# Later weight stores, a second PSUM bank for one transpose, and a moved ones product in an attention and feed-forward kernel

## The chip, the cores and the metric

The kernel runs on one core of a Trainium2 chip. The metric is device time in microseconds (us).

## The reference

Eight batches of attention with normalised queries and keys (12 heads, 448 positions, width 64), then a feed-forward block with squared ReLU, all in fp32 (the weights are handed in as doubles).

```python
def attention(q, k, v, g_q, g_k):            # (8, 12, 448, 64)
    rmsnorm = lambda x, g: x / np.sqrt(np.mean(x * x, axis=-1, keepdims=True) + 1e-06) * g
    scores = np.matmul(rmsnorm(q, g_q), rmsnorm(k, g_k).transpose(0, 1, 3, 2)) / np.sqrt(64)
    attn = np.exp(scores - np.max(scores, axis=-1, keepdims=True))
    return np.matmul(attn / (np.sum(attn, axis=-1, keepdims=True) + 1e-09), v)

x = attention(...).transpose(0, 2, 1, 3).reshape(3584, 768)
h = np.maximum(x @ w_in, 0.0)                # w_in (768, 2048)
return (h * h) @ w_out                       # w_out (2048, 768)
```

## The kernel before

The heads are worked through in pairs; a "pair" below is two heads of one batch, and pairs 0 to 11 are the first two batches. They run alone, by `attention_alone`. At the same time the weights are converted from doubles, block by block, in steps of a quarter tick ("prepare" has four parts, divided by `yield`), and each finished pair of blocks is stored to DRAM, seven sums and differences of it together (1344 KB). From then on the two matrix products of two batches at a time run on TensorE, with attention of the next two batches between the matmuls of the second product. The products fetch their weight blocks (192 KB) from DRAM into five buffers.

```python
def prepare(t):                                   # tick t
    if t == 0: unsigned(0)
    n = t - 3                                     # first quarter: the store of blocks n-1, n
    if there(n) and n % 2:
        c = n % NFC // 2
        dst = w1s[c] if n < NFC else w2s[:, c // 4, :, c % 4]
        nc.sync.dma_start(dst.rearrange("k p m -> p k m"), blocks_of(n)[:, 0:7])
        written[0] = n + 1
    # ... cut: clamp of the exponents of t on VectorE
    yield
    # ... cut: low words on ScalarE, shift on VectorE, first loads
    yield
    # ... cut: merge of bits on VectorE
    total(t - 2, S3, A11, A21, ALU.subtract)      # GpSimd; total() is for odd n only
    total(t - 2, S4, A12, S2, ALU.subtract)
    value(t - 1, 0)                               # GpSimd
    yield
    unsigned(t + 1)                               # ScalarE
    value(t - 1, 1)
    total(t - 1, S1, A21, A22, ALU.add)
    total(t - 1, S2, S1, A11, ALU.subtract)
    load_words(t, t - 1)                          # SP queue
    yield

def transpose(i, s, n):                           # n: which of two PSUM banks
    pt = bank("pt", n)
    for j in range(NJ):
        nc.tensor.transpose(pt[:, j * SP:(j + 1) * SP], normed[i][s][:, j * P:(j + 1) * P], ident[:SP, :SP])
    # ... cut: ScalarE copies pt to qkT

def values(i, chunks=range(NJ)):                  # pav of an odd pair lies in bank 1
    if 0 in chunks:
        pavs[i] = ps_o.tile([P, S], F32, tag="o", name="pav") if i >= NAT or i % 2 == 0 else bank("pav", 1)
    # ... cut: two matmuls for each chunk

def attention_alone():                            # NAT = 12 pairs
    for i in range(NAT):
        more = i + 1 < NAT
        if 0 < i < NAT - 3: load(i + 3)
        scores(i, 0)
        scores(i, 1)
        # ... cut: pair 0
        if more: transpose(i + 1, 1, 0)
        values(i - 1, (2, 3))
        add_up(i, 1)                              # VectorE
        if i + 2 < NAT: norm(i + 2)
        elif not more:
            norm(NAT)
            load(NAT + 2)                         # pair 14, waits until pair 12 is used
        yield                                     # after each yield: a step or two of prepare
        if more: transpose(i + 1, 0, 0)
        load_v(i + 1)
        yield
        scores(i, 2)
        scores(i, 3)
        total_of(i - 1)                           # the ones product: sums of the rows
        values(i, (0, 1))
        finish(i - 1)
        yield
        if added(i) == 3: add_up(i, 2)
        combine_x(i - 1)
        if NAT <= i + 3 < NAT + 2: load(i + 3)
        yield
    values(i, (2, 3))
    total_of(i)
    finish(i)
    combine_x(i)

for u, _ in enumerate(attention_alone()):         # EARLY = 52 steps, 13 ticks
    weights(min(EARLY, 4 + (EARLY - 4) * u // (4 * NAT - 7)))
    if u == 4 * NAT - 9:
        load_blocks(5)                            # the first five weight blocks of the product
```

## Time and profile before

| | before |
|---|---|
| time, median of the first 3 runs | 1401.57 us |
| span of the profiled run | 1399.7 us |
| TensorE busy | 1379.2 us (99%) |
| 75 to 115 us: GpSimd busy | over 19.5 of each 20 us |
| second weight block of the first product starts | 138.18 us |

A line of the timeline reads: start, duration, engine, source line, operation, output and input by name, shapes, count, and in brackets how long the engine was idle before it and what ended that. PE is TensorE, DVE VectorE, ACT ScalarE, POOL GpSimd, SPq the queue from which SP issues transfers. The trace counts each fp32 matmul twice: a weight block of three matmuls is x6.

In the names, pt is a transpose of queries or keys, sc the scores, tot the ones product, pav the values product, pa to pd the sums of the first product, sw a weight block, w1s and w2s the stored weights in DRAM; gT and gC hold probabilities, their sums and weights under conversion until the products need them.

### The profile page before, as it was taken

What the parts mean: (1) busy time and instruction counts of PE and PEld (TensorE: products, weight loads), DVE (VectorE), ACT (ScalarE), POOL (GpSimd) and SP (SyncE); (2) the same over time, 40 slices, a digit from 0 to 9 for tenths busy, and PEclk for the clock granted to TensorE, in tenths of its full rate; (3) what the DMA queues carried; (4) which work ended last, traced back from release to release, by engine and by line L of the source; (5) the groups of instructions that cost most, each with busy time, mean ns of one, the idle gap of its engine ahead of it and who ended that gap; (6) DMA issues with size and microseconds to landing.
All of it is one profiled execution on the core that took longest, in us unless ns stands there. A gap on an engine that the chain in (4) does not pass through costs nothing.

```text
span 1399.7 us, 14445 instructions
## 1 busy us (share of the span) xinstructions
PE 1379.2 (99%) x4450; PEld 638.5 (46%) x4450; DVE 802.2 (57%) x1398; ACT 419.6 (30%) x621; POOL 581.7 (42%) x400
## 2 busy tenths in 40 slices
PE   8989999999999999999999999999999999999997
PEld 3333455444444454544444455444444445554553
DVE  6889676589876234476777523457777633332111
ACT  7875556432322011233332011233333201110000
POOL 5998877444552123544453122544445302221000
PEclk9999999999999999999999999999999999999999
DMA  9687998545764332344665333344564332334443
GB/s 240 189 229 199 341 384 306 143 97 120 144 121 105 102 90 85 104 113 110 127 130 119 97 94 90 98 106 105 129 126 102 95 101 85 90 87 104 106 111 70
DMA packets 430915, 188.79 MB, mean 135 GB/s; under 512 B 277484, under 2 KB 428780, under 8 KB 430828
## 3 DMA queue, kind: packets, MB, share of 16 engines
q1 hardware_dynamic: 421228, 179.05, 49.8%
q10 hardware_dynamic: 9472, 8.72, 2.3%
q8 instruction: 38, 0.62, 0.2%
q14 instruction: 49, 0.40, 0.1%
q0 software_dynamic: 128, 0.00, 0.0%
HBM read 154.54 MB, written 33.16 MB: 134 GB/s over the span
## 4 chain that ended last, share of the span: by engine, by line
PE 93%; POOL 3%; DVE 1%; DMA 1%; ACT 1%; issue 1%; ACTq 0%; POOLq 0%
PE ps L1047 37%; PE sc L749 10%; PE pd L1000 10%; PE pa L1000 10%; PE pc L1000 10%; PE pav L805 9%; PE pb L1000 5%; PE tot L819 1%; POOL rstd L697 1%; POOL gC L563 1%; DMA sw<-w1s 1%; POOL gC L569 1%; PE pt L737 0%; ACT gT L754 0%; POOL qk L699 0%
## 5 line engine op out<-in xcount | busy, mean ns | idle before, releaser
L1047 PE MATMUL ps<-gT,sw 128*128 128x448 f32 x768 | 299.2, 543 | 0.8 <-POOL gT L977 0.8
L719 POOL TENSOR_TENSOR half<-half,mhalf 128x28 f32<-128x28 f32 x36 | 173.6, 4822 | 266.9 <-DVE half L718 226.8
L1047 PE MATMUL ps<-gC,sw 128*128 128x448 f32 x576 | 225.2, 543 | 0.0
L977 POOL TENSOR_TENSOR gT<-gT 128x448 f32<-128x448 f32 x96 | 94.9, 990 | 309.9 <-ACT gT L973 309.9
L1047 PEld LDWEIGHTS ps<-gT,sw 128*128 128x128 f32 x768 | 144.1, 190 | 150.7 <-issue 147.0
L756 ACT ACTIVATE pr<-sc 112x896 f32<-112x896 f32 x120 | 104.7, 914 | 293.4 <-PE sc L749 184.9
L749 PE MATMUL sc<-qkT 64*112 64x448 f32 x768 | 170.6, 563 | 0.9 <-ACT qkT L383 0.8
L1047 PEld LDWEIGHTS ps<-gC,sw 128*128 128x128 f32 x576 | 108.2, 190 | 112.1 <-issue 110.8
L1000 PE MATMUL pa<-xT,sw 128*128 128x448 f32 x384 | 154.9, 540 | 0.0
L973 ACT ACTIVATE gT<-gT 128x448 f32<-128x448 f32 x96 | 55.3, 577 | 310.1 <-DVE gT L1015 310.0
L749 PEld LDWEIGHTS sc<-qkT 64*112 64x112 f32 x768 | 61.2, 173 | 97.9 <-issue 81.3
L1000 PEld LDWEIGHTS pa<-xT,sw 128*128 128x128 f32 x384 | 73.0, 190 | 71.6 <-issue 70.3
L805 PE MATMUL pav<-pr,vt 112*64 112x448 f32 x480 | 100.2, 547 | 0.0
L721 POOL TENSOR_TENSOR qk<-qk,half 128x448 f32<-128x448 f32 x72 | 81.3, 1150 | 2.8
L764 DVE TENSOR_TENSOR acc<-acc,pr 112x896 f32<-112x896 f32 x60 | 68.2, 1136 | 21.0 <-ACT pr L756 18.5
L1000 PE MATMUL pb<-xC,sw 128*128 128x448 f32 x192 | 77.6, 540 | 1.5 <-issue 1.5
L1000 PE MATMUL pd<-xT,sw 128*128 128x448 f32 x192 | 77.9, 542 | 0.0
L1000 PE MATMUL pc<-xC,sw 128*128 128x448 f32 x192 | 77.5, 540 | 0.2 <-DMA sw<-w1s 0.2
L1000 PE MATMUL pd<-xC,sw 128*128 128x448 f32 x192 | 77.5, 540 | 0.0
L1000 PE MATMUL pc<-xT,sw 128*128 128x448 f32 x192 | 77.4, 539 | 0.0
L1015 DVE TENSOR_TENSOR gT<-z,pd 128x448 f32<-128x448 f32 x32 | 19.8, 620 | 99.7 <-PE pd L1000 99.7
L569 POOL TENSOR_TENSOR gC<-gC 128x384 f32<-128x384 f32 x64 | 72.8, 1157 | 2.5
(120 smaller groups left out, 1551.0 us busy)
## 6 DMA issues: line engine op xcount, KB each, us to landing
sw<-w1s SPq DMA_DIRECT2D x224, 192.0 KB, 2.3
sw<-w2s SPq DMA_DIRECT2D x168, 256.0 KB, 3.3
w1s<-gC SPq DMA_DIRECT2D x8, 1344.0 KB, 7.5
w2s<-gC SPq DMA_DIRECT2D x8, 1344.0 KB, 7.6
out_dram<-osb SPq DMA_DIRECT2D x184, 56.0 KB, 1.9
qk<-in_q_dram SPq DMA_DIRECT2D x144, 56.0 KB, 3.0
qk<-in_k_dram SPq DMA_DIRECT2D x144, 56.0 KB, 2.9
vt<-in_v_dram SPq DMA_DIRECT2D x72, 112.0 KB, 2.9
```

The source lines that it names most:

```text
L569: nc.gpsimd.tensor_tensor(*[blocks_of(n)[:, i] for i in (dst, x, y)], op)
L719: nc.gpsimd.tensor_tensor(half, half, mhalf, ALU.pow)
L721: nc.gpsimd.tensor_tensor(qkn[:, s], raw[:, s], half[:, s * NG:(s + 1) * NG].rearrange("p g -> p g ()").to_broadcast([P, NG, 32]), ALU.mult)
L749: nc.tensor.matmul(sc[:, h, 0:S], qkT[rows, at, 1, c * SP:(c + 1) * SP], qkT[rows, at, 0, :], start=True, stop=True)
L756: nc.scalar.activation(pr, sc[:, :, 0:S], AF.Exp)
L764: nc.vector.tensor_tensor(acc, probs[i, 0] if c == 1 else acc, probs[i, c], ALU.add)
L805: nc.tensor.matmul(pavs[i][h * D:(h + 1) * D, :], vs[i][:, h, c, :], probs[i, c][:, h, :], start=(c == 0), stop=(c == NJ - 1))
L973: nc.scalar.activation(g, src, AF.Relu)
L977: nc.gpsimd.tensor_tensor(g, g, g, ALU.mult)
L1000: nc.tensor.matmul(ps, stream[n + i][:, c], rhs[:, c], start=first and c == 0, stop=c == HC - 1, skip_group_check=not first)
L1015: add(g, x, ps, ALU.add)
L1047: nc.tensor.matmul(ps, stream[n][:, c % 4], rhs_of[i][:, c], start=c == 0, stop=c == HF - 1)
```

## The change

Three moves, with no instruction added or removed. The stores go to the third quarter of a tick, so that the SP queue does not stand waiting for GpSimd's last difference. The second transpose of a pair takes the other PSUM bank where pav does not lie there. And the last ones product goes between the last values.

```diff
         if t == 0:
             unsigned(0)
-        n = t - 3
-        if there(n) and n % 2:
-            c = n % NFC // 2
-            dst = w1s[c] if n < NFC else w2s[:, c // 4, :, c % 4]
-            nc.sync.dma_start(dst.rearrange("k p m -> p k m"), blocks_of(n)[:, 0:7])
-            written[0] = n + 1
         if there(t) and doubles:
             e, eu, low, high = parts(t)
@@
         if t < 3:
             load_words(t, t - 1)
         yield
+
+        n = t - 3
+        if there(n) and n % 2:
+            c = n % NFC // 2
+            dst = w1s[c] if n < NFC else w2s[:, c // 4, :, c % 4]
+            nc.sync.dma_start(dst.rearrange("k p m -> p k m"), blocks_of(n)[:, 0:7])
+            written[0] = n + 1
@@
             if more:
-                transpose(i + 1, 0, 0)
+                transpose(i + 1, 0, i % 2)
@@
-        values(i, (2, 3))
+        values(i, (2,))
         total_of(i)
+        values(i, (3,))
         finish(i)
```

## The prediction

> **What bounds the kernel now.** I read the page first, then busy time by stretch, the chain of waits, and the timelines of TensorE, of the SP queue and of the other engines in the first 165 us.
>
> ```profile
> PE 1379.2 (99%) x4450; PEld 638.5 (46%) x4450; DVE 802.2 (57%) x1398; ACT 419.6 (30%) x621; POOL 581.7 (42%) x400
> ```
>
> TensorE is busy 1379.2 of 1399.7 us, so all idle time together is 20.5 us, 1.5%: no rearrangement that leaves the matmuls alone can win 2%. By stretch, TensorE is never idle between 158 and 1260 us. What can move lies before 158 us: the attention of the first two batches (to 134 us), which also converts the weights, and the start of the first product. After that everything only slides along. The first idle spot, from TensorE's timeline (start, duration, line, count, idle before and its releaser):
>
> ```profile
> 17.72 1.73 PE L805 MATMUL pav<-gT,vt 112*64 112x448 f32 x8
> 21.36 0.60 PE L737 MATMUL pt<-ident,qk 112*128 112x112 f32 x4 [1.91 <-ACT qkT L739]
> 21.89 2.97 PE L749 MATMUL sc<-qkT 64*112 64x448 f32 x8
> 24.79 2.91 PE L819 MATMUL tot<-gT,ones 112*64 112x448 f32 x12
> ```
>
> The transpose waits 1.91 us for ScalarE to copy the other transpose out of the same PSUM bank. The next scores and sums are then slow (2.97 and 2.91 us; their like take 1.76 and 2.48). Busy time by stretch shows why, in the column before the DMA share, the granted clock:
>
> ```profile
> 21.00:22.00 1.00, 0.64 (x6) 0.51 (x8) 0.96 (x2) 1.00 (x2) 1.00 (x1) 1.00 1.10 346
> 23.00:24.00 1.00, 1.00 (x6) 0.32 (x2) 1.00 (x2) 1.00 (x3) 0.00 (x0) 0.50 1.09 346
> ```
>
> From about 22.2 to 25.6 us the clock is at half. From about 40 to 115 us GpSimd is the bound (19.0 to 19.8 of each 20 us, but for one gap of 0.54 us): it holds up the transposes by 0.5, 1.45, 2.25 and 0.22 us. From 119.08 to 138.1 us the chain is VectorE's, nearly back to back; the second block of the first product (pb, at 138.18) waits for its last read of the bank of pav.
>
> **What the Trainium skill says.** "TensorE: Matmul & The Clock Gate", Part 1, has a clock of half or full, set by activity in free-running windows of about 3.4 us. The trace agrees: one dip of some 3.4 us to 0.50. The page counts an idle window; here 1.91 us of idling beside short transposes was enough. "PSUM — Partial Sum Buffer", PSUM bank collisions, asks that two engines be kept apart by bank; the 1.91 us wait is that guard. "DMA: Bandwidth & Descriptors", Queues, rings and completion order, says that an engine's ring is consumed in order. The trace fits: a 192 KB weight block, 2.3 us to landing in the median, took 9.39 us at 147.47, behind a 768 KB load and a 1344 KB store.
>
> **Part by part.** No instruction is added or removed: three things move.
>
> **The second bank** (transpose of q when i is odd). At i=1 the transpose can start when pav ends (19.45); its input is ready at 19.26 (VectorE, 18.57 + 0.69), and bank n is free. So the 1.91 us go, and probably the dip: 3.4 us at half clock is 1.7 us of work. Scores, waiting 0.1 us for their buffer, end at 21.8, the sum of ones at 24.2. VectorE, whose read of that sum began at 27.75, is then free at 25.51, so it gains 2.2 us, not 3.6. Followed on through the norm of pair 4 (squares on ScalarE, reduce on VectorE), the pow on GpSimd that began at 35.37 begins at about 32.9. From there GpSimd's own work binds; the 0.54 us gap at 56.09 closes as well, as TensorE is further ahead than that. The gain at 115 us is therefore 2.2 to 3.0 us, **2.7 us** taken. In later odd pairs a pav matmul lies between the two transposes, no wait is seen there, and nothing is won.
>
> **Ones product between the last values.** At 127.81 the values take 3.1 us, then the ones product waits 0.82 us for VectorE to read the former total out of its single buffer (131.10 + 0.64), and runs from 131.80. With half the values after it, it waits from 129.4 to the same 131.8; the other half ends at 135.8 and the first product's pa at 138.1. pb starts at 138.18 either way, for VectorE reaches the last total only at 135.49, after the work of the pair before. So **0 us**: 1.45 us of idling in front of pb moves in front of the ones product.
>
> **Stores half a tick later** (third quarter of four). The trace of the SP queue says which stores wait: SP issues the first five at 52.45, 74.88, 88.66, 107.52 and 123.44, each within 0.08 us of GpSimd's last subtraction. It stood still 37.5 us on them in all. But what stands behind is mostly not urgent: GpSimd is saturated regardless. So the freed queue gives about 0. The fifth store matters:
>
> ```profile
> 123.44 0.38 SPq L583 DMA_DIRECT2D w1s<-gC  x1
> 123.88 4.27 SPq L646 DMA_DIRECT2D sw<-w1s  x5
> 128.24 2.29 SPq L665 DMA_DIRECT2D qk<-in_q_dram  x4
> 130.93 4.46 SPq L665 DMA_DIRECT2D qk<-in_k_dram  x4
> 136.90 1.88 SPq L665 DMA_DIRECT2D qk<-in_q_dram  x4
> 138.88 1.99 SPq L665 DMA_DIRECT2D qk<-in_k_dram  x4
> 140.91 0.48 SPq L535 DMA_DIRECT2D gT<-in_moe_w_out_dram  x1
> 141.48 0.91 SPq L682 DMA_DIRECT2D vt<-in_v_dram  x2
> 142.49 3.05 SPq L646 DMA_DIRECT2D sw<-w1s  x4
> ```
>
> Its new step is number 51 of the 52 that attention runs (12 ticks of 4, and 3). The formula in the code gives 50 steps by the last yield of pair 10, and 52 after the first of pair 11. Before that yield stands the load of pair 14 (136.90), which waits for GpSimd to have used pair 12. So the store goes from 123.44 to about 140.9, 17 us later, right ahead of the 768 KB words, of v, and of the four weight blocks. Block 5, issued at 142.49, landed 4.7 us later, at 147.19, and its matmuls began at 147.35: no slack. With 1344 KB more ahead of it at the 240 to 330 GB/s of these stretches it lands 4.1 to 5.6 us later; pb and GpSimd move alike, so the need stays relative to the issue. The ring was lightly loaded just before, which may help: **a wait of about 3.7 us**. An idle spell of that length probably costs a second dip, 1.7 us at odds of three in four: **1.3 us**. The present wait of 0.19 us at 156.9 goes. In the first product the later stores make GpSimd wait for its buffers, but TensorE does not need those weights yet; the last store leaves one block later (2.25 us), with some 6 us to spare.
>
> Sum: -2.7 + 0 + 3.7 + 1.3 - 0.2 = +2.1 us, to 1403.7. I shade it to **1403.0**, because the gain is read more surely than the stall.
>
> **Rivals.**
>
> **Only the gain.** If the store slips in without delaying block 5 (faster draining, for nothing else is in flight at 140), the time is 1401.6 - 2.7 = 1398.9. For it: weight blocks right behind the store at 123.44 landed in 6.3 to 6.9 us. Against it: even 6.3 us is 1.5 us too late for block 5, and words lie ahead as well.
>
> **GpSimd gains nothing.** If its saturated stretch does not start earlier, or timed runs do not have the dip, the gain falls to about 0.5 us: with the stall and its dip, 1406. Against: GpSimd waited 4.63 us for the norm that follows; the profiled run took 1401.51, as the timed ones.
>
> **GpSimd waits for the later stores within attention** and passes it on. Its next write to the same buffer comes some 20 us after a store (52.45, then 74.80), against 7.5 us to landing. Only the fifth store comes near: next write 144.98, landing about 148. That is 3 us on GpSimd when it no longer bounds; 0 on the time.
>
> **Range and chances.** Low end: the gain alone with a little more, 1398.4; high end: little gain, the stall with its dip, 1406.4. None of this comes near 28 us: faster by over 2% 0.01, within 2% 0.98, slower 0.01.
>
> **What would show it.** The wait of 1.91 us at 21.36 and the half clock at 22 to 26 us gone; the pow of pair 4 near 33 instead of 35.37; pb 2 to 3 us earlier than 138.18; the ones product waiting some 2.4 us and pb hardly at all; the fifth store behind the load of pair 14 and ahead of words; weight block 5 landing 8 to 10 us after issue, with an idle spell of 3 to 5 us on TensorE near 145, perhaps a dip. I am wrong if that block lands in time, or if a clock dip elsewhere (the 2.25 us gap at 95) takes or gives another 1.7 us.

## More of the kernel before

The profile of a kernel is one further execution of it.

The prediction shows the lines of before on which it rests. Three more matter later: two sums of probabilities on VectorE (one of pair 1, one of pair 2), and on GpSimd its first additions for the weights and a pow (timelines of the two engines of the kernel before):

```profile
31.48 2.10 DVE L764 TENSOR_TENSOR gT<-gT 112x896 f32<-112x896 f32 x2
```

```profile
28.75 2.00 POOL L563 TENSOR_TENSOR gC<-gC 128x384 int32<-128x384 int32 x2
35.37 3.14 POOL L697 TENSOR_TENSOR rstd<-rstd,mhalf 112x16 f32<-112x16 f32 x1 [4.63 <-PE sc L749]
```

They do not overlap: GpSimd's two additions end at 30.75, VectorE's two sums start at 31.48 and take 1.05 us each. The third line is the pow of the norm of pair 4 (the inverse square roots of its mean squares), from which GpSimd's saturated stretch runs on.

## The result

| | before | after |
|---|---|---|
| median of 4 runs | 1401.60 us (1400.85 to 1404.35) | 1405.27 us (1404.62 to 1406.70) |
| span of the profiled run | 1399.7 us | 1403.5 us |
| TensorE busy | 1379.2 us | 1380.4 us |
| second block of the first product | 138.18 us | 137.03 us |
| sixth block of the first product | 147.35 us | 150.05 us |

The ratio is 1.0024, with a 95% interval of 1.0007 to 1.0041: within 2%, but slower. The time lies in the predicted range, 2.3 us above the 1403.0 that I had named.

The first idle spot is gone, and with it the half clock. Timeline of TensorE, kernel after:

```profile
17.92 1.72 PE L806 MATMUL pav<-gT,vt 112*64 112x448 f32 x8
19.61 0.57 PE L738 MATMUL pt<-ident,qk 112*128 112x112 f32 x4
20.11 2.04 PE L750 MATMUL sc<-qkT 64*112 64x448 f32 x8
22.09 2.48 PE L820 MATMUL tot<-gT,ones 112*64 112x448 f32 x12
```

The transpose follows pav at once, the scores have 2.04 us instead of 2.97 and the ones product 2.48 instead of 2.91. At the hand-over to the first product the same view shows the loss:

```profile
130.62 2.48 PE L820 MATMUL tot<-gT,ones 112*64 112x448 f32 x12 [1.59 <-DVE gT L833]
132.92 0.92 PE L806 MATMUL pav<-gT,vt 112*64 112x448 f32 x4
...
137.03 2.52 PE L1002 MATMUL pb<-xC,sw 128*128 128x448 f32 x6 [0.73 <-DVE xT L840]
...
150.05 3.44 PE L1002 MATMUL pd<-xC,sw 128*128 128x448 f32 x6 [3.73 <-DMA sw<-w1s]
153.28 3.21 PE L1002 MATMUL pc<-xT,sw 128*128 128x448 f32 x6
```

The second block starts 1.15 us sooner than before. The sixth (block 5 of the prediction, which counts from 0) waits 3.73 us for its weights, and it and the seventh then take 3.44 and 3.21 us instead of 2.4 to 2.5. Busy time by stretch, kernel after (the columns after the stretch are its length, the busy time of TensorE, of its weight loads, of VectorE, ScalarE and GpSimd, each with a count, the granted clock, the DMA share and GB/s), shows the second spell of half clock:

```profile
148.00:150.00 2.00, 0.00 (x0) 0.00 (x0) 0.87 (x1) 0.63 (x1) 2.00 (x3) 1.00 1.12 333
152.00:154.00 2.00, 2.00 (x3) 0.80 (x3) 0.47 (x1) 0.00 (x0) 2.00 (x3) 0.50 1.02 387
```

And the SP queue of the kernel after, where the fifth store was issued at 123.44 before:

```profile
122.47 3.71 SPq L666 DMA_DIRECT2D qk<-in_k_dram  x4
135.72 1.88 SPq L666 DMA_DIRECT2D qk<-in_q_dram  x4
137.69 2.00 SPq L666 DMA_DIRECT2D qk<-in_k_dram  x4
139.74 0.48 SPq L596 DMA_DIRECT2D w1s<-gC  x1
140.26 0.56 SPq L535 DMA_DIRECT2D gT<-in_moe_w_out_dram  x1
140.92 2.42 SPq L683 DMA_DIRECT2D vt<-in_v_dram  x2
143.44 2.82 SPq L647 DMA_DIRECT2D sw<-w1s  x4
```

The queue stands for 9.5 us on the load of pair 14 (issued at 135.72), and the store comes out behind it at 139.74, directly ahead of the words, of v and of weight blocks 6 to 9. The chain of waits of the kernel after ends the wait with `143.44 6.48 DMA sw<-w1s`: the sixth block is issued at 143.44 and lands at 149.92. Two things delay it against the second block. Issuing v takes 2.42 us instead of 0.91, so the block is issued 0.95 us later than before on the trace's clock, where all else is 1.15 us sooner; and it takes 6.5 us to land instead of 4.7.

The trace's account of the 3.9 us: -1.15 at the second block; +3.85 at the sixth (150.05 against 147.35 - 1.15); +1.70 at the ninth (158.59 against 154.19 - 1.15 + 3.85); -0.47 at the tenth (160.84 against 156.91 + 4.40), where the kernel before had a short wait for weights. Sum 3.93, with spans 3.8 us apart.

### The profile page after: what moved, and what is told of

The parts are those of the page before. It is cut to its first block, busy times and chain, and to the rows that moved or that the text cites. A ratio compares the mean times of both kernels' runs of the same rounds, so it can differ in the third digit from the quotient of the medians.

```text
span 1403.5 us, 14447 instructions
## 1 busy us (share of the span) xinstructions
PE 1380.4 (98%) x4450; PEld 638.6 (45%) x4450; DVE 804.9 (57%) x1398; ACT 419.7 (30%) x621; POOL 583.7 (42%) x400
## 4 chain that ended last, share of the span: by engine, by line
PE 92%; POOL 3%; DVE 2%; DMA 1%; ACT 1%; issue 1%; SPq 0%; ACTq 0%; POOLq 0%; DVEq 0%
PE ps L1049 37%; PE pd L1002 10%; PE pc L1002 10%; PE pa L1002 10%; PE sc L750 10%; PE pav L806 9%; PE pb L1002 5%; POOL rstd L698 1%; POOL gC L569 1%; POOL gC L563 1%; PE tot L820 1%; DMA qk<-in_k_dram 1%; POOL qk L700 1%; DMA sw<-w1s 0%; ACT gT L755 0%
## 5 line engine op out<-in xcount | busy, mean ns | idle before, releaser
L722 POOL TENSOR_TENSOR qk<-qk,half 128x448 f32<-128x448 f32 x72 | 84.4, 1191 | 2.8
```

What stands on the lines that cost most here:

```text
L722: nc.gpsimd.tensor_tensor(qkn[:, s], raw[:, s], half[:, s * NG:(s + 1) * NG].rearrange("p g -> p g ()").to_broadcast([P, NG, 32]), ALU.mult)
```

## The experiments

The theory after the result: the fifth store alone, through its place behind the load of pair 14, makes the wait and the half clock, at a cost of about 5 us; the bank gains about 1.2 us; the ones product nothing. The rivals: late stores cost in themselves; part of the loss comes from the other two parts; the half clock has nothing to do with the wait. Runs of one kernel turned out to spread over as much as 3 to 5.5 us, so that effects of 1 us are read from the traces, and the reason for the spread became a question too. Eleven kernels were run, all with a correct result, in three groups; the kernels of a group ran on the same chip. The second group (e5 to e8) and the third (e10 to e12) shared a chip and the runs of the kernel before.

### The three parts alone, and the whole without its late stores

```diff
 e1: before with   transpose(i + 1, 0, i % 2)      only
 e2: before with   the store in the third quarter  only
 e3: before with   values(i, (2,)); total_of(i); values(i, (3,))  only
 e4: before with   the edits of e1 and e3
```

> Only the second bank for the transpose, on the kernel before. Theory (this part gains a little, the late stores lose): the 1.91 us wait and the half clock near 22 us are gone, GpSimd's pow of pair 4 starts 0.4 to 0.7 us earlier than 35.37, the second block of the first product starts about 1.2 us earlier than 138.18, and the time is 1400.2 to 1400.6 us, 1.2 us under before. Rival (the prediction's size, which the stores spoilt in the whole change): 2.7 us under before, 1398.9. Rival (the bank itself costs something later): 1402 or more.

> Only the stores half a tick later. Theory: the fifth store comes behind the load of pair 14 and right ahead of the words; the sixth weight block of the first product lands 3.5 to 4.5 us late, a second spell of half clock follows, and the time is 1406.0 to 1407.0 us, 4.4 to 5.4 over before. Rival (the stall needs the earlier TensorE of the new bank): the stall is under 2.5 us and the time under 1404.5.

> Only the ones product between the last values. Theory: the wait ahead of the ones product grows from 0.8 to about 2.4 us, the wait of 1.45 us ahead of the second block of the first product vanishes, that block starts at 138.2 as before, and the time stays within 0.4 us of before (1401.6). Rival (it frees or delays VectorE): more than 0.5 us either way.

> The whole change without its late stores. Theory: like the bank alone, 1400.2 to 1400.6 us; the parts add up, so the late stores cost 4.7 to 5.1 us of the changed kernel. Rival (part of the loss comes from the new order of the ones product once TensorE is earlier): over 1401.

| kernel | median (6 runs) | ratio to before, 95% interval | second block starts | sixth block waits |
|---|---|---|---|---|
| before (11 runs) | 1402.29 | | 138.18 | 0 |
| e1, bank | 1401.11 | 0.9997, 0.9984 to 1.0009 | 136.95 | 0 |
| e2, stores | 1406.47 | 1.0027, 1.0015 to 1.0039 | 138.22 | 3.83 us |
| e3, ones product | 1401.46 | 0.9995, 0.9983 to 1.0007 | 139.98 | 0 |
| e4, bank and ones | 1401.66 | 1.0003, 0.9989 to 1.0016 | 136.94 | 0 |

The stores alone lose about as much as the whole change did in its own group (e2: 1406.47, a ratio of 1.0027 against 1.0024), with the wait and the half clock both there. Timeline of TensorE of e2:

```profile
151.30 4.02 PE L1001 MATMUL pd<-xC,sw 128*128 128x448 f32 x6 [3.83 <-DMA sw<-w1s]
```

The expected range of e2 was 1406.0 to 1407.0; it holds, and the rival that needs the earlier TensorE falls. The bank's 1.2 us is in the traces of e1 and e4 (second block at 136.95 and 136.94), not in their timed ratios: those runs spread from 1400.2 to 1404.9, and both intervals contain 1. As timed runs, e1, e3 and e4 are inconclusive: the medians of e1 and e4 lie above the 1400.2 to 1400.6 that I expected, and e4's lies above its rival's line of 1401; it is e4's trace, with the second block where e1 has it, that speaks against that rival. In e3 the ones product waits 1.58 us instead of 0.82 and the second block 0.74 instead of 1.45: one wait for the other, as expected in kind. But its second block started 1.8 us late, and the reason lies before anything that the edit changes. Stretches of before, then of e3:

```profile
96.00:99.00 3.00, 3.00 (x16) 1.14 (x18) 2.75 (x2) 2.96 (x6) 2.92 (x3) 1.00 1.17 297
```

```profile
96.00:99.00 3.00, 3.00 (x10) 1.01 (x12) 2.83 (x2) 2.66 (x5) 2.92 (x3) 0.58 1.12 277
```

In both kernels TensorE had just waited for GpSimd for the same 2.2 us (2.25 and 2.23). In the one profiled run the clock fell to half afterwards, in the other it did not. The same happened in the profiled runs of two later kernels: at 95 us in e6, after a wait of 2.22 us, and at 61 us in e7, after one of 1.62 us. Of the eleven traces that have the wait near 95 (2.04 to 2.26 us), e3 and e6 show half clock after it; of the five that have 1.5 us or more near 60, e7 alone.

### Which store, and why

In e5 the fifth store alone stays in the first quarter, the others are late. In e6 all stores are late, but the load of pair 14 is moved behind the step that issues the fifth store.

```diff
 e5:
+        if there(n) and n % 2 and n == 9:      # first quarter
+            ...                                # the store as before
-        if there(n) and n % 2:                 # third quarter
+        if there(n) and n % 2 and n != 9:
 e6:
                 norm(NAT)
-                load(NAT + 2)
             yield
+            if not more:
+                load(NAT + 2)
```

> The changed kernel, but the fifth store alone stays at its old place; the other fifteen leave half a tick later. Theory (one store does all the harm): no wait of over 0.5 us for a weight block near 147 us, no half clock there, and a time as without any late store, 1400.2 to 1401.7 us. Rival (late stores as such cost, through GpSimd's waits for its buffers or a fuller queue): 1403 or more.

> The changed kernel with all stores late, but the load of pair 14 is put behind the step that holds the fifth store and the words. Theory (the store is late only because it stands behind a load that waits for GpSimd): the fifth store is issued by 128 us, the sixth weight block lands in time, and the time is 1400.2 to 1401.7 us. Rival (the stores' place in the tick is what matters): the wait of some 3.7 us stays, 1405.

Both bring the time back: e5 1400.21 us (ratio to before 0.9982, interval 0.9969 to 0.9995), e6 1401.30 us (0.9983, 0.9970 to 0.9997), against 1403.10 us for the kernel before in the same group. Neither trace has a wait for a weight block in the first product. In e6 the fifth store is still late in the tick but is issued before the load of pair 14 (SP queue of e6):

```profile
128.74 0.43 SPq L596 DMA_DIRECT2D w1s<-gC  x1
...
137.71 1.89 SPq L666 DMA_DIRECT2D qk<-in_q_dram  x4
```

I had expected 128; it came at 128.74. So it is not the place in the tick that costs but the place behind a blocked load in an in-order queue, for one store of sixteen. The rival that late stores cost in themselves falls. (e6's profiled run, 1401.76, holds the half clock at 95 us named above, over 30 us before its fifth store.)

### Does the wait cause the half clock?

e7 is the changed kernel with five matmuls of no use in the wait of 3.7 us, into a bank that nobody reads.

```diff
+                if span == 0 and f == 0 and i == A12:
+                    for _ in range(5):
+                        nc.tensor.matmul(both[:, 1, 0:S], xT[:, 0, 0, 0:P], xT[:, 0, 0], start=True, stop=True)
```

(`both` is the two-bank tile of which pa uses the first bank.)

> The changed kernel with five matmuls of no use (0.75 us each, into a bank that is free) between the fifth and the sixth weight block of the first product, where TensorE waits 3.7 us. Theory (the wait also costs a spell of half clock): the sixth block still starts near 150 us, the half clock after it is gone, the ninth block starts 1.5 to 1.7 us sooner than 158.59, and the time falls by about that to 1403.7. Rival (the spell comes from a window that the wait doesn't decide): the half clock stays and the time is 1405 or more.

Timeline of TensorE of e7:

```profile
147.24 3.92 PE L1007 MATMUL pa<-xT 128*128 128x448 f32 x10
151.00 2.42 PE L1003 MATMUL pd<-xC,sw 128*128 128x448 f32 x6
```

The sixth block starts no sooner, seen from the second (12.88 us after it; 13.02 in the changed kernel), but it runs at full speed (2.42 us), and so does the next, at 153.25. From second to ninth block it is 19.64 us, against 21.56 in the changed kernel: 1.9 us, somewhat more than the 1.5 to 1.7 expected. The timed median, 1405.05, is above the 1403.7 that I gave; but the kernel before was at 1403.1 in this group, and the ratio is 1.0013 (1.0000 to 1.0026) instead of 1.0024 and 1.0027 for the changed kernel and e2 in theirs, intervals that overlap. So the trace shows the cause, and the timed runs leave it open. The profiled run had its own spell of half clock at about 61 to 64 us, which is why the expected block time (158.59 less 1.5 to 1.7) is not compared directly.

e12 asks the same of the first wait. It is the kernel before with two such matmuls ahead of the transpose at 21.36; the wait for the bank stays.

```diff
+            if i == 1:
+                idle = bank("idle", 1)
+                for _ in range(2):
+                    nc.tensor.matmul(idle, qkT[:, 0, 0, 0:P], qkT[:, 0, 0], start=True, stop=True)
             if more:
                 transpose(i + 1, 0, 0)
```

> The kernel before, with two matmuls of no use (0.75 us each, into the free bank) in the 1.91 us wait ahead of the transpose at 21.36; the wait itself stays. Theory (the half clock made the bank's gain as much as the wait did, and VectorE and GpSimd cap both): the transpose still starts near 21.4, the scores after it take 1.8 us instead of 2.97 and the ones product 2.5 instead of 2.91, the read of the sum on VectorE starts near 26.1 instead of 27.75, and the pow of pair 4 at 34.7 to 35.0: most of what the bank gained. Rival (the wait is what counts): the pow stays at 35.2 or later.

```profile
19.45 1.77 PE L891 MATMUL idle<-qkT 128*128 128x448 f32 x4
21.45 0.60 PE L737 MATMUL pt<-ident,qk 112*128 112x112 f32 x4 [0.23 <-ACT qkT L739]
21.98 1.76 PE L749 MATMUL sc<-qkT 64*112 64x448 f32 x8
23.67 2.48 PE L819 MATMUL tot<-gT,ones 112*64 112x448 f32 x12
```

The transpose starts as late as before (21.45), yet the pow of pair 4 starts at 34.78 (e1: 34.75) and the second block at 137.01 (e1: 136.95). In these traces, keeping the clock up gains, downstream, all that the second bank gains. All three traces in which that wait is not filled (before, e2, e3) have half clock after it. Median 1400.96, ratio 0.9986 (0.9974 to 0.9999).

### Where the rest of the bank's gain went

The pow of pair 4 was to start 2.4 us sooner and started 0.5 us sooner (34.89 in the changed kernel). Timelines of VectorE and GpSimd of the changed kernel:

```profile
29.74 3.73 DVE L765 TENSOR_TENSOR gT<-gT 112x896 f32<-112x896 f32 x2
```

```profile
28.95 3.57 POOL L563 TENSOR_TENSOR gC<-gC 128x384 int32<-128x384 int32 x2
34.89 3.14 POOL L698 TENSOR_TENSOR rstd<-rstd,mhalf 112x16 f32<-112x16 f32 x1 [2.37 <-DVE rstd L696]
```

VectorE reached its two sums 1.7 us sooner, beside GpSimd's two additions, and both took longer: VectorE's from 2.10 to 3.73 us for two, GpSimd's from 2.00 to 3.57. e8 tests this: GpSimd's additions move into its idle time ahead of the norm of pair 3. It is e4 with

```diff
-        value(t - 1, 0)
+        if t != 1:
+            value(t - 1, 0)
         yield
         unsigned(t + 1)
-        value(t - 1, 1)
+        if t != 1:
+            value(t - 1, 1)
+        if t == 0:
+            value(0, 0)
+            value(0, 1)
```

> Bank and ones product without the late stores, and GpSimd's two sums for the first weight word are placed ahead of the norm of pair 3, into its idle time of 2.5 us, instead of after it. They ran at 28.95 to 32.5 us beside two sums on VectorE, which took 1.87 us each there and 1.05 before. Theory (the gain of the bank shrank from 2.4 to 0.7 us because VectorE and GpSimd now worked at once): VectorE's two sums near 30 us take 1.1 us each again, the pow of pair 4 starts at 33.0 to 33.7 instead of 34.7, and the second block of the first product 1.0 to 1.7 us before 136.9; time 1398.6 to 1399.6. Rival (the sums are slow for another reason): they stay at 1.9 us and the pow of pair 4 stays after 34.4.

Timelines of VectorE and of GpSimd of e8:

```profile
29.99 2.08 DVE L769 TENSOR_TENSOR gT<-gT 112x896 f32<-112x896 f32 x2
```

```profile
22.13 2.74 POOL L563 TENSOR_TENSOR gC<-gC 128x384 int32<-128x384 int32 x2 [0.24 <-issue]
...
33.48 3.14 POOL L702 TENSOR_TENSOR rstd<-rstd,mhalf 112x16 f32<-112x16 f32 x1 [4.23 <-DVE rstd L700]
```

The same sums at the same time take 1.04 us each again, the pow starts at 33.48 and the second block at 135.74, all as the theory has it. The loss came from the overlap of the two engines. The Trainium skill, "GPSIMD Engine Reference", 1. Specifications, says that GpSimd shares its SBUF interfaces with VectorE and contends with VectorE instructions that have two SBUF inputs; the traces agree: the sums have two, and they are slow beside GpSimd only. The median is 1400.60, above my 1398.6 to 1399.6; one of the six runs took 1398.74 and one 1404.02.

### The spread between runs

e10 is e8 with one, one and two matmuls of no use in the three longest waits for GpSimd (ahead of the transposes of q in pairs 5, 7 and 8 of the loop), into the bank of the transpose itself. e11 adds the late stores, the fifth excepted.

```diff
-    def transpose(i, s, n):
+    def transpose(i, s, n, idle=0):
         pt = bank("pt", n)
+        for _ in range(idle):
+            nc.tensor.matmul(pt, xT[:, 0, 0, 0:P], xT[:, 0, 0], start=True, stop=True)
@@
-                transpose(i + 1, 0, i % 2)
+                transpose(i + 1, 0, i % 2, {5: 1, 7: 1, 8: 2}.get(i, 0))
```

> The last run's kernel (bank, ones product, GpSimd's first sums moved, stores as before) with one, one and two matmuls of no use in the three longest waits for GpSimd in attention (0.9, 1.45 and 2.24 us). Theory (the spread of some 3 to 5 us between runs of one kernel is half clock after such waits, in some runs): no half clock before 1390 us in the trace, the second block of the first product within 0.3 us of 135.74, and timed runs of 1398 to 1400 us with a median near 1398.8. Rival (the spread has another source): the runs still reach from 1398.7 to 1404.

> The same with the stores half a tick later but for the fifth, which stays. Theory: without the fifth store the move is worth little, 0 to 0.4 us (the small waits for weight blocks near 145 to 157 us): median 1398.4 to 1398.9. Rival (late stores without the fifth are a gain by themselves): more than 0.8 us under the kernel of the same batch with the stores as before.

| kernel, same group | runs | lowest to highest | median | ratio to before, 95% interval |
|---|---|---|---|---|
| before | 12 | 1401.43 to 1405.61 | 1402.88 | |
| e8 | 6 | 1398.74 to 1404.02 | 1400.60 | 0.9987, 0.9973 to 1.0001 |
| e10 | 5 | 1399.70 to 1400.84 | 1400.45 | 0.9979, 0.9966 to 0.9992 |
| e11 | 4 | 1398.33 to 1398.79 | 1398.56 | 0.9968, 0.9953 to 0.9983 |

The spread falls from 4 to 5 us to 1.1 and 0.5 us. All that e10 adds is work in three waits, so this points to the waits; but four and five runs are few, and e7, which fills none of the three, spread by only 0.83 us in five runs (1404.52 to 1405.35). That the spread is half clock after such waits, in some runs, is shown by the traces of e3, e6 and e7 for single runs, and is inferred for the rest. The mean clocks of the timed runs point the same way, though they are given to 0.001, which is 1.4 us here: in the first group, the three runs of before at 0.995 and 0.996 took 1403.09 to 1405.18 us, the four at 0.998 and 0.999 took 1399.68 to 1402.44. The level of e10 missed my expectation by 1.6 us, and its second block, at 136.13, by 0.1 us; the late stores of e11 bring more than I allowed for: 1.9 us. The rival's bound of 0.8 us is passed. Of this, 1.03 us are two waits for weight blocks which e10 has and e11 has not (timeline of TensorE of e10):

```profile
155.03 2.52 PE L1008 MATMUL pc<-xC,sw 128*128 128x448 f32 x6 [0.41 <-DMA sw<-w1s]
...
228.17 2.52 PE L1008 MATMUL pc<-xT,sw 128*128 128x448 f32 x6 [0.62 <-DMA sw<-w1s]
```

Ahead of the second, e10's SP queue issued a load of words (216.79) and a store (217.83) back to back; in e11 a weight block lies between them (215.78, 217.55, 217.96). That this spacing is the reason was not tested by itself. But all seven traces with every store early (before, e1, e3, e4, e8, e10, e12) show a wait for a weight block in the first product, of 0.17 to 0.64 us, and e5, e6 and e11, with all or all but the fifth late, show none. Another 0.22 us were there at the second block already (VectorE runs 0.26 us later in e10 from 23 us on, before any store), and about 0.6 us are not accounted for.

e11 is the best of all: 4.3 us under the median of before in its group, and 0.46 us from its fastest to its slowest run.

## Why the prediction was right

The time lay in the range, and slower than before, as said. The range of 8 us was wide enough to hold the rival "only the gain" (1398.9) as well, so that the time alone says little; the mechanism is what was right. By its own steps:

- **TensorE bound, only the first 158 us can move.** Right for this change: the two traces are 3.93 us apart at the tenth block and 3.8 at the end. Not in general: e1 and e10 wait 0.64 and 0.62 us for weights at 176 and 228 us.
- **The second bank removes the wait and the half clock.** Right (traces of after and e1). **Its gain of 2.2 to 3.0 us, 2.7 taken**, was mis-sized: 1.15 us in the changed kernel, 1.23 in e1. The term that failed is the pow of pair 4 "at about 32.9": I gave VectorE's two sums their old 1.05 us each, and they took 1.87 beside GpSimd's additions. e8, which takes the overlap away, has the pow at 33.48 and 2.44 us at the second block. The gap at 56.09 closed, as said.
- **Ones product: 0 us.** Right in e3's and e4's traces; the timed runs can't resolve it. I lengthened the wait by twice too much (from 0.82 to "some 2.4" us): I read the 3.1 us of values as two chunks and moved half of them, but they are four chunks in a row, of which one moves (0.77 us), and the wait grew to 1.59. So pb kept a wait of 0.73 us.
- **Fifth store behind the load of pair 14, at about 140.9.** Right: 139.74, in a trace that runs 1.15 us ahead of before there, so 140.9. e5 and e6, which change this store's place alone or the load ahead of it, have no wait.
- **A wait of about 3.7 us.** Right in size, 3.73 us, but partly by luck. I had the block issued in time and landing 4.1 to 5.6 us later for the 1344 KB ahead of it, and took a little off. Landing took only 1.8 us longer (6.5 us, not 8 to 10), and the issue, which I had left in place, came 2.1 us later relative to the second block, 1.5 us of it because v took longer to issue. The two errors cancelled.
- **A second half clock, 1.7 us at three in four.** It came, at 1.70 us, and e7 removes it.
- **Nothing gained by the freed queue elsewhere, but for 0.2 us.** Too little: without the fifth store the late stores are a gain of 1.9 us (e11 against e10), 1.03 us of it traced to short waits for weights in the first product. I had looked for gains in attention, and for that one wait.
- **GpSimd waits for the later stores, without effect.** Right: 2.34 and 3.22 us of such waits near 146 and 158 us in the changed kernel.

The sum was +2.1 us by my terms, shaded to +1.4; measured, +3.7. The bank's 1.5 us and the odds on the half clock (0.4 us) make up most of the difference. The shading went the wrong way: I took the gain to be read more surely than the stall, and it was the stall that came as read, while less than half of the gain came.

## What to carry to other kernels

In an in-order queue, moving an issue by a little in the program can move it by 16 us in time if a blocked transfer lies between: check for each instance what now stands ahead of it and what now stands behind it. A wait of TensorE of 1.6 to 2.2 us cost some 1.7 us more in clock here, in some runs only, so that filling waits with matmuls of no use can pay; that it also narrows the spread of the timings is likely from e10 and e11, and not shown. And when one engine starts sooner, look up what the other engines do at that moment before using its old durations.

## What the Trainium skill lacked or had wrong

- "TensorE: Matmul & The Clock Gate", 🎯 Why this matters for your kernels, advises to avoid idle gaps of more than about 3 us. Here gaps of 1.62 us (e7, at 60), 1.91 us (before, at 21.36) and 2.23 us (e3, at 95) were followed by some 3.4 us at half clock; the gap of 2.25 us at 95 in the trace of before was not. The runs show no threshold, only that gaps of this size do it in some runs.
- No page says whether such waits, within a kernel, make its timings spread (the TensorE page speaks of varying runs only for the slow matmuls at a kernel's start): 1401.43 to 1405.61 us for before, 1398.33 to 1398.79 for a version with the waits filled (e11). The runs suggest it and do not show it.
- "GPSIMD Engine Reference", 1. Specifications, names the contention with VectorE but gives no size, and the rule on "SBUF — State Buffer", Who interferes with whom, comes without a time for such a pair: two-input sums on VectorE (112x896) went from 1.05 to 1.87 us each, GpSimd's additions (128x384) from 1.0 to 1.8.
- "DMA: Bandwidth & Descriptors", Queues, rings and completion order, has rings that are consumed in order but gives no size for the wait behind a large transfer: 192 KB took 6.5 us behind a store of 1344 KB, 768 KB of words and v, and 9.39 us at 147.47 in before, against a median of 2.3. Nor does it say that issuing slows: v took 2.42 us to issue instead of 0.91.
